# An attention and MLP kernel on one core: its work items broken into single instructions, with a newly written order

## The chip, the cores and the metric

The kernel runs on one core of one Trainium2 chip. The metric is the device time of one execution in microseconds (us), as the median of several runs. The core has five engines that run side by side, each through its own queue in the order written: PE (TensorE: matmul and transpose), DVE (VectorE), ACT (ScalarE), POOL (GpSimd) and SP (SyncE, which here issues all DMAs). An engine whose next instruction waits for another engine does nothing else meanwhile.

## The reference

Inputs are q, k, v of shape (4, 8, 576, 64), a tiny network that makes a position bias, and the weights of an MLP with 512 inputs and 2048 hidden units. All is float32.

```python
scores = scale * np.matmul(q, k.transpose(0, 1, 3, 2))
x = (psi_rel / psi_i)[..., None]          # log1p|i-j| / log1p(max(i,1))
h = np.maximum(x @ w1 + b1, 0.0)          # 32 hidden units
bias = h @ w2                             # one value per (i, j, head)
scores = scores + bias.transpose(2, 0, 1)[None, :, :, :]
attn = exp(scores - max); attn = attn / (sum + 1e-09)
attn_out = np.matmul(attn, v)             # then (B*S, H*D) = (2304, 512)
h = np.maximum(x @ w_in, 0.0)
out = h * h @ w_out
```

## The kernel before

Every float32 operand of a large matmul is split into a float16 high part and a float16 rest, and three float16 matmuls take the place of one float32 matmul. The work is cut into items, and `PROGRAM` is a list of words, each naming one item (kind and numbers). The kinds:

- Bias: `hg:g.j` (min or max of a table row, on DVE and ACT, L444 and L440) makes the hidden layer for group g of 16 rows, `bm:g.c` multiplies it by w2 on PE (L501), `bo` writes it out of PSUM (ACT L520, DVE L525) and by DMA to `biasd` in DRAM, and `bl:n` loads the slice of step n. There are 36 groups.
- Weights: `wd:i` loads a piece of 128 x 512 double-precision words, `ws:i` makes float16 halves of it: three steps on DVE (L348, L349, L351), a cast on ACT (L260), a scale and a subtraction on POOL. There are 32 pieces; MLP unit u of every block needs pieces 4u to 4u+3.
- Attention: 80 steps n, one head of two batches and up to 128 rows each. `qk:n` makes scores in the one PSUM buffer `sc` (PE L561, L566, L571), `sa:n` adds the bias and takes the maximum on DVE (L588, which frees `sc` for the next step) and the exponential on ACT (L597), then the weights are transposed: in steps 0 to 15 by PE (`tu:n.b`, L610 and L615, copied out of PSUM by ACT, L611 and L616), later by DMA after a split on ACT and POOL (`sb:n`). `pv:n` multiplies by V on PE (L660; float32 in steps 0 to 15, where each such matmul leaves two records in the trace). `po:k` divides four heads' results by the sums (DVE L674, L676).
- MLP: ten blocks of eight steps each. `no:k` scales a block (DVE L691 and others), `tx:k.b` splits it on DVE (L704, L705) and transposes it by DMA, `g1:n` is the first matmul of unit n (24 records, L719), `sq:n` squares with relu (ACT L732, DVE L733, DVE L264, POOL L736), `g2:n` the second matmul (12 matmuls, 6 in the half blocks, L750), `ou` stores.

Two PSUM buffers `h` serve `bm`, `tu` and `g1` in turn: the third of them can begin only when the first has been copied out. Buffers are handed out in the order of the words.

After all instructions are recorded, a table `STREAMS` holds a permutation of each engine's instructions (PE 5712, ACT 693, DVE 692, POOL 385, SP 376), and a chain of order-only dependences fixes that order. So engine order is already free of the words' order; the buffers are not. The core of it:

```python
for word in PROGRAM.split():
    kind, _, arg = word.partition(":")
    work[kind](*[int(x) for x in arg.split(".") if x])
...
        for prev, i in zip(seq, seq[1:]):
            tc.add_manual_dep(i, prev.name, mybir.DependencyInfo(
                mybir.DependencyClass.NoSync, mybir.DependencyReason.DATA), reason="order")
```

Of the kernel before, what the change touches and what calls it, by code (L numbers as in the profile page):

```python
# [44 lines left out]
NF = 2  # L45
PROGRAM = (
    "st tb:0 qd:0 tb:1 wd:0 wd:1 sc hc kd:0.0 hg:0.0 wd:2 hg:0.1 kd:0.1 hg:1.0 vd:0.0 vd:0.1 hg:2.0 hg:1.1 vd:0.2 "
    "bm:0.1 vd:0.3 hg:2.1 vd:0.4 bm:1.1 vd:0.5 qs:0 vd:0.6 bo:0.1.0 hg:3.0 hg:3.1 rs bm:0.0 bo:0.0.0 bm:1.0 ks:0.0 "
    "bm:2.0 vd:0.7 bm:2.1 bo:1.0.0 bo:1.1.0 bm:3.1 bo:2.0.0 bm:3.0 ks:0.1 bo:2.1.0 kz:0.0 qk:0 kd:0.2 bo:3.0.0 "
    "bo:3.1.0 qd:1 ws:0 hg:4.0 hg:4.1 bm:4.0 kz:0.1 kd:0.3 ws:1 wd:3 hg:5.0 hg:5.1 bm:5.0 bo:4.0.0 bo:4.0.1 wd:4 "  # L50
    "bo:5.0.0 bo:5.0.1 ws:2 hg:6.0 hg:6.1 bm:6.0 ks:0.2 bl:0 bl:1 wd:5 kz:0.2 bo:6.0.0 bl:2 qs:1 bo:6.0.1 hg:7.0 "
    "kd:0.4 ks:0.3 ws:3 qd:2 hg:7.1 bm:7.0 kz:0.3 kd:0.5 wd:6 sa:0 bo:7.0.0 bo:7.0.1 ws:4 qk:1 bl:3 hg:8.0 hg:8.1 "
    "sa:1 tu:0.0 wd:7 bl:4 ws:5 tu:0.1 tu:1.0 ks:0.4 wd:8 tu:1.1 qk:2 kz:0.4 kd:0.6 bm:8.0 ks:0.5 sa:2 pv:0 "
    "bo:8.0.0 pv:1 bo:8.0.1 ws:6 bl:5 hg:9.0 qk:3 hg:9.1 wd:9 tu:2.0 qs:2 kd:0.7 kz:0.5 sa:3 tu:2.1 bm:9.0 bl:6 "
    "qk:4 bo:9.0.0 bo:9.0.1 ws:7 pv:2 ks:0.6 hg:10.0 qd:3 hg:10.1 bm:10.0 wd:10 kz:0.6 sa:4 tu:3.0 bo:10.0.0 bl:7 "
    "bo:10.0.1 ws:8 tu:3.1 hg:11.0 hg:11.1 qk:5 pv:3 po:0 wd:11 ws:9 bm:11.0 sa:5 ks:0.7 qk:6 bo:11.0.0 tu:4.0 "
    "bo:11.0.1 wd:12 ws:10 tu:4.1 sa:6 pv:4 hg:12.0 qk:7 hg:12.1 wd:13 bm:12.0 qs:3 kz:0.7 bl:8 tu:5.0 bl:9 "
    "bo:12.0.0 qd:4 tu:5.1 bo:12.0.1 ws:11 tu:6.0 sa:7 wd:14 ws:12 qk:8 hg:13.0 hg:13.1 bl:10 tu:6.1 pv:5 bm:13.0 "
    "pv:6 sa:8 wd:15 bo:13.0.0 tu:7.0 bo:13.0.1 ws:13 hg:14.0 tu:7.1 qk:9 bl:11 hg:14.1 pv:7 wd:16 bm:14.0 sa:9 "
    "tu:8.0 bo:14.0.0 tu:8.2 bo:14.0.1 ws:14 qk:10 bl:12 hg:15.0 hg:15.1 wd:17 tu:8.1 bm:15.0 sa:10 po:1 bo:15.0.0 "  # L60
    "ws:15 bo:15.0.1 wd:18 ws:16 qk:11 hg:16.0 bl:13 hg:16.1 bm:16.0 qs:4 wd:19 tu:9.0 qd:5 bo:16.0.0 bo:16.0.1 "
    "ws:17 tu:9.2 no:0 hg:17.0 tu:9.1 hg:17.1 wd:20 ws:18 tu:10.0 tu:10.2 pv:8 vs:0.0 sa:11 wd:21 ws:19 tx:0.0 "
    "tu:10.1 pv:9 ws:20 wd:22 bl:14 bm:17.0 tu:11.0 bo:17.0.0 wd:23 vs:0.1 tu:11.2 bo:17.0.1 ws:21 qk:12 hg:18.0 "
    "hg:18.1 tu:11.1 wd:24 g1:0 sa:12 bm:18.0 sq:0 ws:22 pv:10 bo:18.0.0 bl:15 bo:18.0.1 ws:23 wd:25 hg:19.0 "
    "hg:19.1 tu:12.0 g1:1 wd:26 vs:0.2 tu:12.1 sq:1 ws:24 qk:13 wd:27 tu:12.2 sa:13 bm:19.0 g2:0 bo:19.0.0 "
    "bo:19.0.1 ws:25 hg:20.0 g1:2 wd:28 hg:20.1 qk:14 bl:16 sq:2 ws:26 g1:3 g2:1 sq:3 sa:14 wd:29 tu:13.0 ws:27 "
    "pv:11 po:2 vs:0.3 bl:17 wd:30 ws:28 tu:13.1 qk:15 tu:13.2 wd:31 bm:20.0 sa:15 g2:2 bo:20.0.0 qs:5 bo:20.0.1 "
    "ws:29 hg:21.0 tu:14.0 bl:18 hg:21.1 tu:14.1 pv:12 vs:0.4 kd:1.0 ws:30 qd:6 qk:16 g2:3 ws:31 kd:1.1 tu:14.2 "
# [795 lines left out]
```

## Time and profile before

| what | value |
|---|---|
| median of 3 runs | 653.91 us (653.08 to 658.23) |
| the profiled execution's own time | 654.47 us |
| its span in the trace | 652.5 us |
| mean granted PE clock | 0.963 |
| busy PE / DVE / ACT / POOL | 616.6 / 417.1 / 380.0 / 379.5 us |

The span is what the trace covers; 2.0 us of the execution's own time lie around it. A busy time is the union of an engine's instructions. [...]

### The profile page before, as it was taken

What the parts mean: (1) busy time and instruction counts of PE and PEld (TensorE: products, weight loads), DVE (VectorE), ACT (ScalarE), POOL (GpSimd) and SP (SyncE); (2) the same over time, 40 slices, a digit from 0 to 9 for tenths busy, and PEclk for the clock granted to TensorE, in tenths of its full rate; (3) what the DMA queues carried; (4) which work ended last, traced back from release to release, by engine and by line L of the source; (5) the groups of instructions that cost most, each with busy time, mean ns of one, the idle gap of its engine ahead of it and who ended that gap; (6) DMA issues with size and microseconds to landing.
All of it is one profiled execution on the core that took longest, in us unless ns stands there. A gap on an engine that the chain in (4) does not pass through costs nothing.

```text
span 652.5 us, 15566 instructions
## 1 busy us (share of the span) xinstructions
PE 616.6 (94%) x6056; PEld 398.4 (61%) x6056; DVE 417.1 (64%) x836; ACT 380.0 (58%) x838; POOL 379.5 (58%) x389
## 2 busy tenths in 40 slices
PE   5686889989999999999999999999999999999997
PEld 2143366756666647666666666766766666767664
DVE  8878987967977895596784456437445642632321
ACT  7689977975854457657654655655565563342111
POOL 5777467998465447678884545647455655342221
PEclk9779968978999999999999999999999999999999
DMA  8999886746996799999977867777787677624000
GB/s 316 305 309 287 288 259 188 245 127 129 187 209 163 149 194 206 162 190 226 255 164 145 188 120 168 156 162 147 149 167 145 147 143 147 131 58 79 17 34 16
DMA packets 206568, 112.16 MB, mean 172 GB/s; under 512 B 167072, under 2 KB 183456, under 8 KB 206496
## 3 DMA queue, kind: packets, MB, share of 16 engines
q1 hardware_dynamic: 206496, 111.19, 72.7%
q8 instruction: 47, 0.77, 0.5%
q14 instruction: 25, 0.20, 0.1%
HBM read 55.44 MB, written 15.61 MB: 109 GB/s over the span
## 4 chain that ended last, share of the span: by engine, by line
PE 63%; DVE 13%; DMA 8%; ACT 8%; issue 4%; POOL 3%; SPq 0%; DVEq 0%; POOLq 0%; ACTq 0%
PE hp L719 23%; PE o L750 22%; PE pv L660 9%; PE sc L571 5%; DMA at<-a 3%; PE bp L501 2%; DVE s L588 2%; DVE hg L444 2%; ACT s L597 2%; POOL a L629 2%; DMA biasd<-be 2%; ACT be L520 1%; ACT hg L440 1%; PE sc L566 1%; DMA stg<-w_in 1%
## 5 line engine op out<-in xcount | busy, mean ns | idle before, releaser
L719 PE MATMUL hp<-xt,winH 128*128 128x256 f16 (+1 forms) x1280 | 195.8, 263 | 0.1
L750 PE MATMUL o<-woutH,g 128*128 128x512 f16 x576 | 185.7, 379 | 0.4 <-POOL g L736 0.4
L736 POOL TENSOR_TENSOR g<-r,g 128x512 f16<-128x512 f32 (+1 forms) x80 | 90.9, 1136 | 139.2 <-DVE g L264 110.0
L719 PE MATMUL hp<-xt,winL 128*128 128x256 f16 (+1 forms) x640 | 162.9, 263 | 0.0
L588 DVE CUSTOM_DVE_ANT_0 s<-sc,bt 128x576 f32<-128x576 f32 x144 | 104.5, 750 | 58.3 <-PE sc L571 25.2
L750 PEld LDWEIGHTS <-g 128*128 128x128 f16 x864 | 82.2, 98 | 92.9 <-issue 8.3
L719 PEld LDWEIGHTS <-winH 128*128 128x128 f16 x1280 | 117.3, 98 | 31.4 <-issue 13.0
L629 POOL TENSOR_TENSOR a<-s,a 128x1024 f16<-128x1024 f32 (+1 forms) x64 | 131.1, 2049 | 0.0
L733 DVE TENSOR_TENSOR r<-hp,r 128x512 f32<-128x512 f32 (+1 forms) x80 | 50.8, 636 | 117.1 <-ACT r L732 116.9
L597 ACT ACTIVATE s<-s,nm 128x576 f32<-128x576 f32 x144 | 111.5, 775 | 6.7
L750 PE MATMUL o<-woutL,g 128*128 128x512 f16 x288 | 109.2, 379 | 0.0
L596 ACT ACTIVATE nm<-mx,esc 128x1 f32<-128x1 f32 x144 | 40.8, 288 | 114.3 <-DVE mx L588 113.8
L660 PE MATMUL pv<-v,at 128*128 128x64 f16 (+5 forms) x2112 | 97.1, 208 | 3.8 <-ACT at L611 3.0
L732 ACT ACTIVATE r<-hp 128x512 f32<-128x512 f32 (+1 forms) x80 | 43.6, 544 | 72.9 <-PE hp L719 72.8
L260 ACT ACTIVATE a<-s 128x1152 f16<-128x1152 f32 (+1 forms) x64 | 70.3, 1098 | 21.0 <-DMA at<-a 20.3
L660 PEld LDWEIGHTS <-at 128*128 128x128 f16 (+1 forms) x1792 | 56.7, 100 | 19.0 <-issue 6.3
L719 PEld LDWEIGHTS <-winL 128*128 128x128 f16 x640 | 63.1, 99 | 5.8
L628 POOL TENSOR_TENSOR a<-s,a 128x128 f16<-128x128 f32 (+1 forms) x64 | 28.5, 445 | 49.0 <-ACT a L260 47.2
L444 DVE TENSOR_SCALAR hg<-tab_t 128x464 f32<-128x464 f32 (+17 forms) x84 | 54.9, 684 | 2.5 <-PE bp L501 2.4
L571 PE MATMUL sc<-k,q 64*128 64x512 f16 x384 | 53.7, 386 | 0.0
L501 PE MATMUL bp<-hg,w2s 128*32 128x288 f32 (+16 forms) x156 | 35.8, 546 | 9.7 <-ACT hg L440 6.5
L660 PEld LDWEIGHTS pv<-v,at 128*64 128x64 f32 (+3 forms) x320 | 33.1, 197 | 11.4 <-ACT at L611 4.1
(88 smaller groups left out, 701.8 us busy)
## 6 DMA issues: line engine op xcount, KB each, us to landing
bt<-biasd SPq DMA_DIRECT2D x64, 288.0 KB, 3.3
stg<-w_in SPq DMA_DIRECT2D x16, 512.0 KB, 5.2
stg<-w_out SPq DMA_DIRECT2D x16, 512.0 KB, 4.8
bt<-biasd SPq DMA_DIRECT2D x32, 144.0 KB, 4.4
qst<-qd SPq DMA_DIRECT2D x32, 128.0 KB, 3.4
out<-o SPq DMA_DIRECT2D x16, 256.0 KB, 2.3
v<-vd SPq DMA_DIRECT2D x8, 320.0 KB, 6.4
stg<-vd SPq DMA_DIRECT2D x8, 320.0 KB, 4.1
```

Of the source, the lines that this page charges most:

```text
L260: nc.scalar.activation(out=out, in_=in_, func=AF.Copy, scale=scale)
L444: nc.vector.tensor_scalar(ht, src, scl[:, n:n + 1], None, op0=ALU.min)
L501: nc.tensor.matmul(out=bp[32 * t:32 * t + 32, 0:n], lhsT=w2s if gi < 4 or t < z else w2n, rhs=hg[gi, t][:, a0:a1, :] if gi in ONEP else hg ...
L571: nc.tensor.matmul(out=sc[:, 1024 * b:1024 * b + 512], lhsT=qt[r, qz, qs], rhs=kt[r, z, 64 * b:64 * b + 512], start=(m == 0), stop=(m == 2 ...
L588: nc.vector.tensor_tensor_reduce(s[:, 576 * b:576 * b + 576], sc[:, 960 * sb:960 * sb + 576], bt, inv, -3.0e38, ALU.add, ALU.max, mx[:, b: ...
L597: nc.scalar.activation(out=sl, in_=sl, func=AF.Exp, bias=nm[:, b:b + 1], accum_out=su[:, h, b:b + 1])
L629: eng.tensor_tensor(av[:, :, 640:1152], ev[:, :, 0:512], av[:, :, 0:512], op=ALU.subtract)
L660: nc.tensor.matmul(out=dst, lhsT=lhsT, rhs=vt[r, 5 * b + blk, :] if f32 else vt[:, vz, 5 * b + blk, :], start=(m == 0), stop=(m == nt - 1) ...
L719: nc.tensor.matmul(out=hp[:, f * T:f * T + T].rearrange("p (b t) -> p b t", b=nb), lhsT=wt[:, k, c0:c0 + 128], rhs=xt[:, 0:nb, z * 4 + k, ...
L733: nc.vector.tensor_tensor(rr, hp[:, 0:2 * T], rr, op=ALU.mult)
L736: eng.tensor_tensor(g[:, 1, 0:2 * T], rr, g[:, 0, 0:2 * T], op=ALU.subtract)
L750: nc.tensor.matmul(out=blk["o"][b], lhsT=g[:, z, c0:c0 + 128], rhs=wt[:, 2 * u + f, :], start=(u == 0 and f == 0 and z == 0 and wt is wout ...
```

## The change

Each item function becomes a generator that stops (`yield`) after an instruction. A word of `PROGRAM` now runs one such unit: the first time it stands there it starts the item, each later time it runs the item's next unit. Most units are one instruction; a run of matmuls (`qk`, `pv`, `g1`, half a `g2`) is still one unit. `PROGRAM` is therefore much longer, `STREAMS` is gone, and each engine runs its instructions in the order in which the words bring them. Buffers are now taken when the unit that first writes them stands in the list. Which engine does what is as before, and so are the pools.

The list `f32c` of the two blocks that use float32 in `pv` becomes a count of steps, `NF = 16`: the same steps. Their `po` now carries V's power of two through the sums (one more tiny constant, `eps[:, 1:2]`, and a scale in an ACT instruction that was there before).

```diff
-NF = 2
+NF = 16
 PROGRAM = (
...
+    "st tb:0 qd:0 st st tb:1 st st st st st st st wd:0 qd:0 qd:0 qd:0 sc hc hc kd:0.0 hc hc hc hc hc kd:0.1 sc rs "
...
-STREAMS = {
-    "PE": (
...
     def softmax_a(n):
...
             nc.vector.tensor_tensor_reduce(
                 s[:, 576 * b:576 * b + 576],
                 sc[:, 960 * sb:960 * sb + 576], bt, inv, -3.0e38, ALU.add, ALU.max, mx[:, b:b + 1])
+            yield
...
     def pv(n):
...
-        f32 = (p, c) in f32c
+        f32 = n < NF
...
     def pv_out(k):
...
+        f32 = 4 * k < NF
+        nc.scalar.activation(out=rd[:, :, 0:nb], in_=su[:, h0:h0 + 4, 0:nb], func=AF.Identity,
+                             scale=float(2.0 ** -VS) if f32 else 1.0, bias=eps[:, 1:2] if f32 else eps[:, 0:1])
+        yield
...
     def square(n):
...
-        g = g_p.tile([128, 2, 512], F16, tag="g", name="g")
         rr = r[:, 0:2 * T]
         nc.scalar.activation(out=rr, in_=hp[:, 0:2 * T], func=AF.Relu, scale=float(2.0 ** (-2 * RS)))
+        yield
         nc.vector.tensor_tensor(rr, hp[:, 0:2 * T], rr, op=ALU.mult)
+        yield
+        g = blk["g"][u] = g_p.tile([128, 2, 512], F16, tag="g", name="g")
...
+    live = {}
     for word in PROGRAM.split():
-        kind, _, arg = word.partition(":")
-        work[kind](*[int(x) for x in arg.split(".") if x])
...
+        if word not in live:
+            kind, _, arg = word.partition(":")
+            live[word] = iter(work[kind](*[int(x) for x in arg.split(".") if x]) or ())
+        next(live[word], None)
```

What the new list does to the order shows at two places. The first is PE's queue at the first steps of the second block. Before, behind `qk:11`: bias group 16 (L501), `tu:9` (L610, L615), the first transposes of `tu:10`, `pv:8` (L660), a last `tu:10`, `pv:9`.

```order
L501 MATMUL bp_1143<-hg_1135,w2s_130 32x384 x2
L501 MATMUL bp_1143<-hg_1140,w2n_132 32x384 x2
L610 MATMUL tp_1154<-ident_140,s_1025 128x128 x4
L615 MATMUL tp_1177<-ident_140,s_1025 64x128 x2
L610 MATMUL tp_1192<-ident_140,s_1025 128x128 x4
L610 MATMUL tp_1212<-ident_140,s_1089 128x128 x4
L615 MATMUL tp_1218<-ident_140,s_1089 64x128 x2
L660 MATMUL pv_1222<-v_193,at_1034 128x64 x10
L610 MATMUL tp_1261<-ident_140,s_1089 128x128 x4
L660 MATMUL pv_1222<-v_195,at_1153 128x64 x10
```

After, the same engine from `tu:8.1` on (L667 and L674 are the transposes, L723 is `pv`, L547 the bias, L615 and L620 `qk`). Up to the first weight load of `qk:11`:

```order
L667 MATMUL tp_1087<-ident_140,s_970 128x128 x4
L723 MATMUL pv_1105<-v_184,at_1066 128x64 x10
L547 MATMUL bp_1128<-hg_1094,w2s_130 32x384 x2
L547 MATMUL bp_1128<-hg_1097,w2n_132 32x384 x2
L667 MATMUL tp_1137<-ident_140,s_1043 128x128 x4
L674 MATMUL tp_1148<-ident_140,s_1043 64x128 x2
L615 LDWEIGHTS q_624
```

and from the end of `qk:11` on, with `tu:9.1`, `pv:9`, bias group 17, `tu:10` and `pv:10`:

```order
L620 MATMUL sc_141<-k_411,q_624 128x512
L667 MATMUL tp_1173<-ident_140,s_1043 128x128 x4
L723 MATMUL pv_1105<-v_192,at_1153 128x64 x10
L547 MATMUL bp_1212<-hg_1185,w2s_130 32x368 x2
L547 MATMUL bp_1212<-hg_1201,w2n_132 32x368 x2
L667 MATMUL tp_1227<-ident_140,s_1123 128x128 x4
L674 MATMUL tp_1235<-ident_140,s_1123 64x128 x2
L667 MATMUL tp_1247<-ident_140,s_1123 128x128 x4
L723 MATMUL pv_1105<-v_202,at_1240 128x64 x10
```

`pv:8` now stands ahead of bias group 16 and directly behind its own transposes, `qk:11` (nine matmuls) stands between the two halves of `tu:9`, and `tu:10` comes after `pv:9`.

The second place is DVE's queue where the softmax of steps 16 to 18 meets the first unit of the second MLP block. Before: the last step of `ws:31` (L351), the two halves of step 16 (L588 on `s_1841`, with three bias rows L444 between them), both halves of step 17 (`s_1924`), then the product of `sq:4` (L733).

```order
L351 SCALAR_TENSOR_TENSOR cv_1822<-stg_1718,ci_1823 128x512
L588 ISA s_1841,mx_1842<-sc_142,bt_1587 128x576
L588 ISA mx_1842 128x1
L444 TENSOR_SCALAR hg_1869<-tab_t_129 128x432
L444 TENSOR_SCALAR hg_1872<-tab_t_129 128x432 x2
L588 ISA s_1841,mx_1842<-sc_142,bt_1587 128x576
L588 ISA mx_1842 128x1
L588 ISA s_1924,mx_1925<-sc_142,bt_1687 128x576
L588 ISA mx_1925 128x1
L588 ISA s_1924,mx_1925<-sc_142,bt_1687 128x576
L588 ISA mx_1925 128x1
L733 TENSOR_TENSOR r_1976<-hp_1940,r_1976 128x256
```

After: `sq:4` (L808) stands ahead, then the last weight steps, bias group 23, the product of `sq:5`, and only then the first half of step 17 (L637 on `s_2022`).

```order
L808 TENSOR_TENSOR r_1923<-hp_1879,r_1923 128x256
L380 SCALAR_TENSOR_TENSOR cv_1940<-stg_1775,ci_1911 128x512
L373 TENSOR_SCALAR ci_1945<-stg_1850 128x512
L375 SCALAR_TENSOR_TENSOR ci_1945<-stg_1850,ci_1945 128x512
L482 TENSOR_SCALAR hg_1955<-tab_t_129 128x448
L380 SCALAR_TENSOR_TENSOR cv_1987<-stg_1850,ci_1945 128x512
L482 TENSOR_SCALAR hg_2002<-tab_t_129 128x448 x2
L743 TENSOR_TENSOR x_1463<-pv_1585,rd_1828 128x256
L808 TENSOR_TENSOR r_2008<-hp_1958,r_2008 128x256
L743 TENSOR_TENSOR x_1463<-pv_1585,rd_1828 128x256
L637 ISA s_2022,mx_2023<-sc_141,bt_1694 128x576
L637 ISA mx_2023 128x1
```

On PE the same place reads, in words, `tu:15.0 tu:15.1 qk:17 tu:15.2 pv:14 g1:4 bm:22 qk:18 g1:5 bm:23 pv:15` before, and `pv:14 qk:16 g2:3 tu:15.1 tu:15.0 tu:15.2 g1:4 bm:22 pv:15 g1:5 qk:17 bm:23` after. From step 40 on the two orders on PE agree but for a few units that change places with near ones.

## Rows read from the trace of the kernel before

**Rows 1.** Busy time of each engine by stage, to 640 us; PEclk is the granted clock.

```profile
core 0: us, PE busy (x) PEld busy (x) DVE busy (x) ACT busy (x) POOL busy (x), PEclk, DMA share, GB/s
0.00:20.00 20.00, 11.56 (x102) 5.31 (x102) 17.29 (x42) 13.43 (x27) 10.09 (x21) 1.00 0.92 328
20.00:40.00 20.00, 13.96 (x48) 4.53 (x46) 14.62 (x25) 13.80 (x33) 14.69 (x16) 0.60 1.00 290
40.00:80.00 40.00, 31.27 (x326) 16.37 (x322) 36.87 (x75) 37.29 (x92) 24.48 (x27) 0.95 0.95 301
80.00:103.00 23.00, 19.30 (x93) 14.39 (x91) 17.54 (x36) 16.13 (x39) 13.89 (x17) 0.63 0.72 214
103.00:136.00 33.00, 32.95 (x303) 23.27 (x302) 31.28 (x59) 26.66 (x64) 31.02 (x41) 1.00 0.74 219
136.00:158.00 22.00, 19.51 (x133) 13.48 (x133) 12.95 (x24) 14.77 (x32) 19.84 (x23) 0.77 0.43 106
158.00:330.00 172.00, 170.10 (x1805) 107.67 (x1805) 134.47 (x258) 105.79 (x233) 111.60 (x105) 1.00 0.92 195
330.00:640.00 310.00, 310.00 (x3195) 208.58 (x3192) 150.61 (x318) 150.67 (x320) 151.84 (x139) 1.00 0.62 127
```

**Rows 2.** Timeline of PE, 81 to 104 us: start, duration, instruction, idle time before it.

```profile
85.17 1.93 PE L610 MATMUL tp<-ident,s 128*128 128x128 f32 x8 [2.32 <-ACT be L520]
...
88.40 4.94 PE L660 MATMUL pv<-v,at 128*128 128x64 f32 x20
93.27 1.11 PE L610 MATMUL tp<-ident,s 128*128 128x128 f32 x4
```

**Rows 3.** Timeline of PE, 104 to 124 us: the same kinds of instruction later.

```profile
105.88 2.86 PE L660 MATMUL pv<-v,at 128*128 128x64 f32 x20
108.67 0.66 PE L610 MATMUL tp<-ident,s 128*128 128x128 f32 x4
```

**Rows 4.** Timeline of ACT, 82 to 85 us.

```profile
82.74 0.79 ACT L597 ACTIVATE s<-s,nm 128x576 f32<-128x576 f32 x1
...
83.50 0.65 ACT L260 ACTIVATE winH<-cv 128x512 f16<-128x512 f32 x1
84.02 1.10 ACT L520 ACTIVATE be<-bp,hcst,rows_s 128x207 f32<-128x207 f32 x2
```

**Rows 5.** The chain of waits, 136 to 160 us: start, duration, what.

```profile
142.49 4.73 PE pv L660 x20
147.22 2.68 PE hp L719 x24
149.90 0.98 PE bp L501 x8
150.88 0.27 PE sc L566 x3
151.15 0.75 PE sc L571 x6
151.90 1.45 PE hp L719 x24
153.35 2.23 PE bp L501 x8
155.58 2.79 PE pv L660 x20
```

**Rows 6.** Who waited for whom, 136 to 158 us: total, times, longest.

```profile
DVE r L733 <- ACT r L732: 6.4, 1, 6.4
...
PE sc L566 <- DVE mx L588: 1.6, 1, 1.6
```

**Rows 7.** What DVE waited for, 20 to 44 us: total, times, longest.

```profile
DVE ci L348 <- DMA stg<-w_out: 3.6, 1, 3.6
DVE q L395 <- POOL q L262: 2.6, 1, 2.6
```

**Rows 8.** Groups of instructions by line and shape: busy time, mean ns of one.

```profile
L351 DVE SCALAR_TENSOR_TENSOR cv<-stg,ci 128x512 uint32<-128x512 uint32 x32 | 21.7, 678 | 0.8 <-DMA biasd<-be 0.5
```

More of the change, by code (lines that the diff above doesn't have):

```diff
@@ L44 @@
 NKZ = 8
-NF = 2
+NF = 16
 PROGRAM = (
[67 rows of a table removed]
-)
-NAMES = {"PE": "PE", "Activation": "ACT", "DVE": "DVE", "Pool": "POOL", "SP": "SP"}
-STREAMS = {
-    "PE": (
-        "0-3 12-19 4-11 20-980 987-1014 981-986 1015-1065 1072-1095 1066-1071 1096-1360 1367-1375 1361-1366 1376-1526 "
-        "1533-1536 1527-1532 1537-2083 2090-2113 2084-2089 2114-2667 2674-2697 2668-2673 2698-3251 3258-3281 3252-3257 "
-        "3282-3835 3842-3865 3836-3841 3866-4419 4426-4449 4420-4425 4450-5711 "
-    ),
-    "ACT": (
[15 rows of a table removed]
-    ),
-    "DVE": (
[16 rows of a table removed]
-    ),
-    "POOL": (
[8 rows of a table removed]
-    ),
[11 rows of a table removed]
-    ),
-}
[153 rows of a table added]
+)
 @with_exitstack
@@ L273, in tile_attention_moe @@
         groups += list(range(32, 36)) if c == 0 else list(range(8 * c - 8, 8 * c))
-    f32c = order[:NF]
     k_t, v_t, q_t, kst, vst, wst, q_st = {}, {}, {}, {}, {}, {}, {}
@@ L577, in softmax_a @@
         bt = b_t.pop(n)
[L578 removed]
+        s = s_t[n] = s_p.tile([128, 1152], F32, tag="w", name="s")
         mx = sml.tile([128, 2], F32, tag="mx", name="mx")
         nm = sml.tile([128, 2], F32, tag="nm", name="nm")
[L581 removed]
+        if (p, c) not in sums:
             sums[p, c] = sml.tile([128, H, 2], F32, tag="sum", name="sum")
@@ L603, in turn, with at_of @@
         e = s_t[n]
-        if b == 0:
-            at_t[n] = as_f32(at_p.tile([128, 20, 128], F16, tag="at", name="at")).rearrange("p (k i) -> p k i", i=128)
-        at = at_t[n]
+        def at_of():
+            if n not in at_t:
+                t = as_f32(at_p.tile([128, 20, 128], F16, tag="at", name="at"))
+                at_t[n] = t.rearrange("p (k i) -> p k i", i=128)
+            return at_t[n]
         if b < nb:
@@ L666, in pv_out @@
         h0 = k % 2 * 4
-        po = pv_t.pop(k)
-        if h0 == 0:
+        su = sums[p, c]
+        rd = sm2.tile([128, 4, 2], F32, tag="rd", name="rd")
+        f32 = 4 * k < NF
+        nc.scalar.activation(out=rd[:, :, 0:nb], in_=su[:, h0:h0 + 4, 0:nb], func=AF.Identity,
+                             scale=float(2.0 ** -VS) if f32 else 1.0, bias=eps[:, 1:2] if f32 else eps[:, 0:1])
+        yield
+        nc.vector.reciprocal(out=rd[:, :, 0:nb], in_=rd[:, :, 0:nb])
+        yield
+        po = pv_t[k]
+        if (p, c) not in x_t:
             x_t[p, c] = x_p.tile([128, 2, DM], F32, tag="x", name="x")
         x = x_t[p, c]
-        su = sums[p, c]
-        rd = sm2.tile([128, 4, 2], F32, tag="rd", name="rd")
-        nc.scalar.activation(out=rd[:, :, 0:nb], in_=su[:, h0:h0 + 4, 0:nb], func=AF.Identity, bias=eps)
-        nc.vector.reciprocal(out=rd[:, :, 0:nb], in_=rd[:, :, 0:nb])
         for b in range(nb):
@@ L743, in g2 @@
         g = blk["g"].pop(u)
-        if u == 0:
-            blk["o"] = [ps_o.tile([128, 512], F32, tag=f"o{b}", name=f"o{b}") for b in range(nb)]
         for b in range(nb):
+            if u == 0:
+                blk["o", b] = ps_o.tile([128, 512], F32, tag=f"o{b}", name=f"o{b}")
             for f in range(2):
@@ L749, in g2 @@
                     c0 = f * T + b * 128
-                    nc.tensor.matmul(out=blk["o"][b], lhsT=g[:, z, c0:c0 + 128], rhs=wt[:, 2 * u + f, :],
+                    nc.tensor.matmul(out=blk["o", b], lhsT=g[:, z, c0:c0 + 128], rhs=wt[:, 2 * u + f, :],
                                      start=(u == 0 and f == 0 and z == 0 and wt is woutH),
                                      stop=(u == 7 and f == 1 and z == 1))
+            if b < nb - 1:
+                yield
     def store(k, b):
@@ L758, in store @@
         if zn("oe", 2 * k + b) == "A":
-            nc.scalar.activation(out=o, in_=blk["o"][b], func=AF.Copy, scale=blk["os"][:, b:b + 1])
+            nc.scalar.activation(out=o, in_=blk["o", b], func=AF.Copy, scale=blk["os"][:, b:b + 1])
         else:
-            nc.vector.tensor_scalar(o, blk["o"][b], blk["os"][:, b:b + 1], None, op0=ALU.mult)
+            nc.vector.tensor_scalar(o, blk["o", b], blk["os"][:, b:b + 1], None, op0=ALU.mult)
+        yield
         if c:
@@ L779, in start @@
                                 compare_op=ALU.is_equal, fill=0.0)
+        yield
         if "T" in ENG["wl"]:
             nc.gpsimd.tensor_scalar(negw, ident, -float(2.0 ** -WIS), 1.0, op0=ALU.mult, op1=ALU.mult)
-        nc.vector.memset(eps, 1.0e-9 * 2.0 ** ESC)
+            yield
+        nc.vector.memset(eps[:, 0:1], 1.0e-9 * 2.0 ** ESC)
+        yield
+        nc.vector.memset(eps[:, 1:2], 1.0e-9 * 2.0 ** (ESC - VS))
+        yield
         nc.vector.memset(esc, ESC * LN2)
+        yield
         nc.scalar.activation(out=nb1, in_=hcst[:, 0:1], func=AF.Exp)
@@ L802, in tile_attention_moe @@
             "ou": store}
+    live = {}
     for word in PROGRAM.split():
-        kind, _, arg = word.partition(":")
-        work[kind](*[int(x) for x in arg.split(".") if x])
-    own = {e: [] for e in STREAMS}
-    for i in nc.cur_bb.bb.instructions:
-        e = NAMES.get(str(i.engine).split(".")[-1])
-        if e and type(i).__name__.startswith("Inst"):
-            own[e].append(i)
-    for e, text in STREAMS.items():
-        seq = []
-        for w in text.split():
-            a, _, b = w.partition("-")
-            seq += own[e][int(a):int(b or a) + 1]
-        assert len(seq) == len(own[e])
-        for prev, i in zip(seq, seq[1:]):
-            tc.add_manual_dep(i, prev.name, mybir.DependencyInfo(
-                mybir.DependencyClass.NoSync, mybir.DependencyReason.DATA), reason="order")
+        if word not in live:
+            kind, _, arg = word.partition(":")
+            live[word] = iter(work[kind](*[int(x) for x in arg.split(".") if x]) or ())
+        next(live[word], None)
+    tail = {}
+    for i in nc.cur_bb.bb.instructions:
+        if type(i).__name__.startswith("Inst"):
+            e = str(i.engine)
+            if e in tail:
+                tc.add_manual_dep(i, tail[e].name, mybir.DependencyInfo(
+                    mybir.DependencyClass.NoSync, mybir.DependencyReason.DATA), reason="order")
+            tail[e] = i
 def kernel(q, k, v, w1, b1, w2, moe_w_in, moe_w_out):
```

95 lines of the change are left out of this document (75 added, 20 removed), and 269 rows, old and new, of tables (PROGRAM, STREAMS).

## The prediction

> **What bounds the kernel now.** I read the busy times by stage first [rows 1]. From 330 to 640 us PE is busy in every microsecond at a granted clock of 1.00, and from 158 to 330 us it lacks 1.9 us in 172. The work of PE does not change, so nothing is to be had in these 482 us but those 1.9; whatever the new order does there, PE has to run through the same matmuls, and DVE, ACT and POOL each have half their time left (150 to 152 us of 310). All that an order can win lies ahead of 158 us. [...]
>
> What PE waits for there is not one engine. From 40 to 80 us DVE (36.9 of 40) and ACT (37.3 of 40) are both nearly full, and the DMA share is 0.95; from 20 to 40 it is 1.00, and DVE waits 3.6 us for a weight load and 2.6 us for a cast on POOL [rows 1, 7]. These stretches are full of work, and I expect little there. The stretches 80 to 103 and 136 to 158 are different: no engine is full (DVE 17.5 of 23 and 13.0 of 22, ACT 16.1 and 14.8), and PE is slow. In the first, PE pauses 2.32 us for ACT's copying out of bias group 16, which frees the PSUM buffer for the next transposes; then eight transposes take 1.93 us, `pv:8` 4.94 us, and another four transposes 1.11 us [rows 2]. The same `pv` takes 2.86 us and the same four transposes 0.66 us at 105 to 109 us [rows 3]. In the second, the chain runs over PE alone: `pv:14` 4.73 us against 2.79 for `pv:15`, `g1:4` 2.68 against 1.45 for `g1:5`, bias group 23 2.23 against 0.98 for group 22 [rows 5]. Meanwhile DVE sits 6.4 us behind the product of `sq:4`, whose matmul stands behind the slow `pv:14`, and `qk:17` had waited 1.6 us for DVE [rows 6]. So here idle time makes a slow clock, and the slow PE makes the others idle.
>
> **The change part by part.** The time of the profiled execution is 654.47 us; its span is 652.5, so 1.97 us lie around it, and the median of the runs, 653.91, is 0.56 below it. A new span counts as itself plus 1.4.
>
> *V's power of two* costs nothing: the same 16 steps use float32 as before, the scale sits in an ACT instruction that was there, and one memset of a single column is added on DVE in the first 3 us, where DVE waits for loads anyway (it is busy 17.3 of 20 [rows 1]). With that cover gone it is one tiny instruction.
>
> *Units in place of items, and buffers taken later* add no instruction to any engine. They matter only through the order, so I price the order at the two places where PE is slow.
>
> *80 to 103 us.* The pause of 2.32 us ended when ACT had copied out bias group 16 at 84.02 us. Ahead of that on ACT stood an exponential of step 10 (from 82.74 to 83.50, 0.76 us) and a weight cast (to 84.02, 0.52 us) [rows 4]. In the new order these two come behind; another cast of the same size (0.52) and a transpose copy of about as much take 1.0 us of their 1.28, so the copying out comes 0.3 us sooner. And PE now has `qk:11` to do between the two halves of `tu:9`: three and six matmuls, 0.27 + 0.75 = 1.02 us [rows 5]. The pause falls to about 2.32 - 1.02 - 0.3 = 1.0 us; regained 1.3. The slow clock behind the pause cost 2.08 us in each of two `pv` (4.94 - 2.86; the second, `pv:9`, has the same 4.94), 0.45 in each of two groups of four transposes (1.11 - 0.66), and 0.6 in the eight (1.93 - 2 x 0.66): 5.7 us [rows 2, 3]. I take it that with `pv:8` ahead of bias group 16 and the pause at 1.0 us the clock holds: 7.0 us for this place. If it falls all the same, 1.3; if the new pauses are no shorter, 0.
>
> [...]
>
> *136 to 158 us.* Before, `qk:17` stood directly behind `tu:15.1` and waited 1.6 us for DVE's second half of step 16 [rows 6]. In the new order PE has `pv:14`, `g1:4`, bias group 22, `pv:15` and `g1:5` ahead of it: 2 x 2.79 + 2 x 1.45 + 0.98 = 9.5 us more work at the full clock [rows 5]. On DVE six steps of the last two weight pieces now come behind step 16, 6 x 0.68 = 4.1 us less ahead of it [rows 8]. So the wait goes, and so does DVE's wait of 6.4 us, since `g1:4` is no longer behind step 17. The slow clock there cost 1.94 + 1.23 + 1.25 = 4.4 us in the three groups above. Other pauses can make the clock fall here, since PE only just became dense, so I take half, 2.2, with the 1.6: 3.8 us. The ends are 0 and 6.0.
>
> What is late next: in the new order `sa:0` and `sa:1` stand seven DVE instructions further back, behind bias groups 8 and 9, and the last weight steps come the 4.1 us later that were counted above. Unit 7 of the first MLP block needs them, and `tu:15`, `g1:4` to `g1:6` and two `pv` still stand ahead of it on PE, so there is room. POOL, which halves the weights and V behind DVE, is nearly full from 103 to 158 us (31.0 of 33, 19.8 of 22 [rows 1]), and nobody in these rows waits long for it. New pauses of PE somewhere I price between 0 (as from 103 to 136, where PE misses 0.05 us in 33) and 5 us; from 40 to 80 us it misses 8.7 in 40, but that stretch exists already. PE's work there grows denser, at the former rate; I take 1.5.
>
> Sum: 652.5 - 7.0 - 3.8 + 1.5 = 643.2 us of span, **644.6 us**.
>
> **The rivals.** *All pauses but the forced ones go.* DVE is idle 158 - (17.3 + 14.6 + 36.9 + 17.5 + 31.3 + 13.0) = 27.4 us ahead of 158 [rows 1]. Forced are 2.7 at the start, the 6.2 for the loads and the cast [rows 7], and 3.1 from 40 to 80 us. If DVE, the engine with the most work there, paces the new order without other gaps, 15.4 us go: a span of 637.1, 638.5 us. For it: PE's work ahead of DVE's at the second place shrinks as shown. Against it: ACT is as full as DVE from 40 to 80.
>
> *The waits only move.* The old order was already set for each instruction of each engine, so the units give no freedom but that of the buffers. The clock falls at other places for as long; only the second place is better: 3.8 us gained and up to 5 lost, a span of 648.7 to 653.7, 650 to 655 us. For it speaks that the stretches to 80 us are full, and that PE's share of busy time ahead of 103 us is low in any order.
>
> *Slower: one more fall of the clock.* PE ran 103 to 136 us at 1.00 with hardly a pause [rows 1]. The new order moves `tu:10`, `tu:12` and `pv:11` to `pv:13` against `g1` and `g2` in just this stretch. If a pause like the 2.32 us arises there, a third slow stretch costs what the first did, 5.7 + 2.3 = 8.0 us, and if the first one stays and the second gains nothing, the span is 660.5, 661.9 us. It decides from a pause of some 2 us that is followed by a `pv` of more than 4 us. Against it: ACT (26.7 of 33) has room there.
>
> **How the numbers follow.** The forecast has a chance of 0.50, all pauses gone 0.15, waits that only move 0.22, one more fall of the clock 0.13. The forecast's own range is 639 to 650 (the 7.0 down to 1.3, the 3.8 up to 6.0, new pauses 0 to 5, not all at once). The range over all reaches from 634, a little under the first rival since part of the load waits could go too, to 656, which takes in the moved waits and leaves out the third rival. A measurement of this kernel can tell about 1% from no change, 6.5 us. Faster by more than that (under 647.4): nine tenths of the forecast and the first rival, 0.60. Within 1%: 0.27. Slower by over 1%: 0.13.
>
> **What would show it.** Right if the clock of the stretch around `pv:8` and `pv:9` is near 1.00 and both take about 2.8 us; if `qk:17` waits for nothing and DVE has no wait of 6 us at `sq:4`; if the 310 us of full PE stand unchanged, only earlier; and if the stretch to 80 us is as before within 2 us. Wrong if a `pv` of float32 steps still takes 4.9 us, if PE pauses for ACT's copying out at other steps, or if DVE waits longer for weight loads ahead of 80 us.

## The result and the profile after

The changed kernel takes 647.28 us (median of 4, 646.23 to 648.05) against 654.25 for the kernel before on the same chip: a ratio of 0.9882 (of the means of the runs), 95% interval 0.9838 to 0.9926. On another chip it was 647.25 against 655.88, 0.9875 (0.9840 to 0.9911). The forecast was 644.6 in a range of 634 to 656. The profiled execution has a span of 645.6 us, 6.9 less than before.

The busy times by stage, which answer to [rows 1] (columns: stretch, its length, busy time and instructions of PE, PEld, DVE, ACT and POOL, granted clock (1.00 is the full clock), DMA share, GB/s):

```profile
0.00:20.00 20.00, 10.69 (x94) 5.07 (x94) 16.44 (x41) 13.10 (x27) 8.87 (x21) 1.00 0.92 321
20.00:40.00 20.00, 12.03 (x38) 2.65 (x38) 16.75 (x27) 12.13 (x27) 14.96 (x17) 0.61 1.00 305
...
80.00:103.00 23.00, 20.67 (x191) 15.68 (x190) 21.82 (x45) 21.58 (x54) 21.52 (x25) 1.00 0.83 239
103.00:136.00 33.00, 31.57 (x276) 21.73 (x275) 29.64 (x57) 26.73 (x63) 31.18 (x41) 1.00 0.71 213
136.00:158.00 22.00, 18.88 (x178) 9.81 (x178) 21.09 (x36) 15.27 (x33) 19.38 (x24) 1.00 0.65 159
158.00:180.00 22.00, 19.14 (x214) 11.80 (x211) 15.77 (x33) 17.90 (x39) 12.42 (x12) 1.00 0.99 204
```

The two slow stretches are gone: the clock from 80 to 103 us is 1.00 (0.63 before), from 136 to 158 us 1.00 (0.77). The slow one from 20 to 40 us stays, at 0.61. The other engines do more in the same time: DVE is busy 21.8 of 23 us in the first (17.5 before) and 21.1 of 22 in the second (13.0). From 330 to 640 us PE is full as before.

The timeline of PE around `pv:8` and `pv:9`, which answers to [rows 2, 3] (the kernel before had 4.94 us for each):

```profile
78.83 1.36 PE L723 MATMUL pv<-v,at 128*128 128x64 f32 x10
80.40 1.47 PE L723 MATMUL pv<-v,at 128*128 128x64 f32 x10 [0.21 <-ACT at L670]
82.58 0.66 PE L667 MATMUL tp<-ident,s 128*128 128x128 f32 x4
...
84.80 1.36 PE L723 MATMUL pv<-v,at 128*128 128x64 f32 x10
86.48 1.47 PE L723 MATMUL pv<-v,at 128*128 128x64 f32 x10 [0.31 <-ACT at L670]
```

Each `pv` is 2.83 us of work (1.36 + 1.47), with a pause of 0.2 or 0.3 us in it, and four transposes take 0.66 us. What PE waited for from 136 to 180 us (total, times, longest), to be read beside [rows 6]:

```profile
PE pv L723 <- DMA at<-a: 2.9, 2, 1.9
PE o L827 <- POOL g L814: 1.8, 2, 1.0
PE o L827 <- POOL g L281: 1.0, 1, 1.0
PE bp L547 <- DVE hg L482: 0.3, 1, 0.3
```

The wait of `qk:17` for DVE is gone, and so is DVE's wait of 6.4 us. In their place PE waits for POOL's halves of the squares and for the transposes by DMA of steps 17 and 19. At the head, the first softmax half of step 0 on DVE (L588 in the kernel before, L637 in the changed one, 0.75 us in both) begins at 31.52 us before and at 37.23 us now.

It comes 5.7 us later. To see what that is worth, and where the 6.9 us came from, I use PE's lag: the time less the work that PE has done by then, where each group of matmuls counts at what it takes undisturbed (of its kind and per matmul, the duration that a quarter of the groups in the traces of before and after stay under). Idle time and a slow clock both add to the lag; work moved about does not, and idle transposes count as no work. In us, with some of the experiments below:

| at | before | changed | e1 old order | e2 first place undone | e3 second undone | e4 old head | e5 old order, pauses filled | e8 first place alone |
|---|---|---|---|---|---|---|---|---|
| 40 | 18.9 | 20.7 | 19.8 | 20.7 | 20.2 | 19.9 | 19.9 | 20.3 |
| 80 | 30.8 | 30.6 | 31.8 | 31.8 | 30.4 | 30.9 | 32.5 | 29.7 |
| 103 | 42.3 | 33.2 | 43.6 | 43.7 | 33.0 | 37.8 | 40.4 | 32.9 |
| 136 | 42.3 | 34.7 | 44.9 | 46.2 | 41.7 | 38.7 | 41.7 | 41.7 |
| 158 | 49.8 | 39.1 | 51.2 | 48.8 | 48.2 | 43.8 | 45.1 | 48.7 |
| 180 | 50.2 | 43.2 | 52.1 | 55.9 | 52.4 | 46.4 | 47.8 | 49.8 |
| 640 | 54.6 | 47.7 | 56.2 | 61.7 | 57.0 | 52.5 | 51.6 | 53.8 |

Against the kernel before, the changed one is level at 80 us (0.2 ahead), gains 8.9 from 80 to 103, loses 1.5 to 136, gains 3.1 to 158 and loses 3.7 to 180; 6.9 remain at the end, the difference of the two spans.

Each column is one execution. In the trace of e9, which is the changed kernel again in an execution of 650.50 us, PE is busy 32.68 us from 40 to 80 us against 35.82 here, so the lag at 80 us can differ by some 3 us between executions of one kernel; from 80 to 103 and from 136 to 158 us the clock is 1.00 there too. The columns e4 and e8 are of executions of 652.15 and 653.86 us, above their medians.

### The profile page after: what moved, and what is told of

Read it like the earlier page. It is cut to its first block, busy times and chain, and to the rows that moved or that the text cites. A ratio compares the mean times of both kernels' runs of the same rounds, so it can differ in the third digit from the quotient of the medians.

```text
span 645.6 us, 15577 instructions
## 1 busy us (share of the span) xinstructions
PE 608.3 (94%) x6056; PEld 388.9 (60%) x6056; DVE 421.3 (65%) x837; ACT 380.9 (59%) x838; POOL 378.3 (59%) x389
## 4 chain that ended last, share of the span: by engine, by line
PE 71%; DMA 9%; ACT 9%; POOL 4%; issue 3%; DVE 3%; SPq 0%; DVEq 0%; POOLq 0%; ACTq 0%
PE o L827 26%; PE hp L794 24%; PE pv L723 8%; PE sc L620 5%; DMA at<-a 4%; PE bp L547 3%; ACT s L649 2%; DMA xt<-xh 2%; ACT be L566 2%; PE sc L610 1%; ACT hg L478 1%; DMA qst<-qd 1%; PE sc L615 1%; DMA stg<-w_out 1%; ACT at L670 1%
## 5 line engine op out<-in xcount | busy, mean ns | idle before, releaser
L814 POOL TENSOR_TENSOR g<-r,g 128x512 f16<-128x512 f32 (+1 forms) x80 | 87.0, 1088 | 116.4 <-DVE g L283 88.3
L637 DVE CUSTOM_DVE_ANT_0 s<-sc,bt 128x576 f32<-128x576 f32 x144 | 104.7, 749 | 46.3 <-PE sc L620 28.8
L808 DVE TENSOR_TENSOR r<-hp,r 128x512 f32<-128x512 f32 (+1 forms) x80 | 50.8, 635 | 120.0 <-ACT r L806 119.9
L723 PE MATMUL pv<-v,at 128*128 128x64 f16 (+5 forms) x2112 | 90.4, 204 | 3.4 <-DMA at<-a 2.9
L723 PEld LDWEIGHTS <-at 128*128 128x128 f16 (+1 forms) x1792 | 56.2, 100 | 20.6 <-issue 7.6
L620 PE MATMUL sc<-k,q 64*128 64x512 f16 x384 | 52.6, 379 | 0.0
L547 PE MATMUL bp<-hg,w2s 128*32 128x288 f32 (+16 forms) x156 | 39.0, 547 | 12.4 <-ACT hg L478 9.0
L283 DVE TENSOR_SCALAR g<-r 128x512 f16<-128x512 f32 (+1 forms) x64 | 38.5, 601 | 2.5 <-DVE r L808 0.5
```

The costliest lines, as they stand in the source:

```text
L547: nc.tensor.matmul(out=bp[32 * t:32 * t + 32, 0:n], lhsT=w2s if gi < 4 or t < z else w2n, rhs=hg[gi, t][:, a0:a1, :] if gi in ONEP else hg ...
L620: nc.tensor.matmul(out=sc[:, 1024 * b:1024 * b + 512], lhsT=qt[r, qz, qs], rhs=kt[r, z, 64 * b:64 * b + 512], start=(m == 0), stop=(m == 2 ...
L637: nc.vector.tensor_tensor_reduce(s[:, 576 * b:576 * b + 576], sc[:, 960 * sb:960 * sb + 576], bt, inv, -3.0e38, ALU.add, ALU.max, mx[:, b: ...
L723: nc.tensor.matmul(out=dst, lhsT=lhsT, rhs=vt[r, 5 * b + blk, :] if f32 else vt[:, vz, 5 * b + blk, :], start=(m == 0), stop=(m == nt - 1) ...
L808: nc.vector.tensor_tensor(rr, hp[:, 0:2 * T], rr, op=ALU.mult)
L814: eng.tensor_tensor(g[:, 1, 0:2 * T], rr, g[:, 0, 0:2 * T], op=ALU.subtract)
```

## The experiments

Theory A: the time is in the order of the engines; at two places it removes the pauses of PE behind which the clock fell. Rival B: taking the buffers later is what gains. Rival C: the later start of step 0 is carried to the end, so that the gain could have been larger. The first four ran on one chip, the next four on another, the last four on a third, each set beside the kernel before. Every run that changes the order moves units of all engines together; none changes PE's order alone.

**e1, the old order in the new units.** The list is sorted so that each engine runs as before (up to a few tiny instructions); units, later buffers and V's power of two stay. On PE, at the first place (- the changed list, + this one, the words of PE alone):

```diff
-tu:8.1 pv:8 bm:16.0 tu:9.0 tu:9.2 qk:11 tu:9.1 pv:9 bm:17.0 tu:10.0
+tu:8.1 bm:15.0 qk:11 bm:16.0 tu:9.0 tu:9.2 tu:9.1 tu:10.0 tu:10.2 pv:8
```

> The changed program (single units, buffers taken at the unit, V's power of two), but its list is sorted so that every engine runs its instructions in the order of the kernel before. Theory A (the time is all in the order of the engines): 652 to 656 us, as before, with the slow pv of 4.9 us at 88 us. Rival B (taking the buffers later is what gains): 647 to 650 us, with shorter pauses in the old order.

Measured: 656.19 us, 1.0028 of before (1.0004 to 1.0053), at the upper end of what theory A gave. B fell: the units and the buffers gain nothing by themselves. The timeline of PE has the old pause and the old slow `pv:8`:

```profile
78.82 0.53 PE L546 MATMUL bp<-hg,w2s 128*32 128x400 f32 x2 [1.21 <-ACT at L669]
...
80.37 0.33 PE L614 MATMUL sc<-kz,q 128*128 128x128 f16 x3 [0.68 <-DVE mx L636]
...
82.84 1.02 PE L546 MATMUL bp<-hg,w2s 128*32 128x384 f32 x3 [1.38 <-ACT hg L477]
...
84.12 0.66 PE L666 MATMUL tp<-ident,s 128*128 128x128 f32 x4
...
87.19 1.14 PE L666 MATMUL tp<-ident,s 128*128 128x128 f32 x8 [2.20 <-ACT be L565]
...
90.44 4.94 PE L722 MATMUL pv<-v,at 128*128 128x64 f32 x20
```

**e2, the first place undone; e3, the second undone.** In the changed list the units between `pv:7` and `pv:11` (e2), or between `pv:13` and the first half of `g2:5` (e3), go back into their old relative order. e2 has on PE what the diff of e1 shows; e3:

```diff
-pv:14 qk:16 g2:3 tu:15.1 tu:15.0 tu:15.2 g1:4 bm:22.0 pv:15 g1:5 qk:17
+qk:16 g2:3 tu:14.2 bm:21.0 tu:15.0 tu:15.1 qk:17 tu:15.2 pv:14 g1:4
```

> The changed kernel with the units between pv:7 and pv:11 put back into the relative order of before (PE: qk:11, bm:16, tu:9, tu:10, then pv:8); the rest of the list as changed. Theory A (the clock falls behind the pause for bias group 16): pv:8 and pv:9 take 4.9 us again and the time is 5 to 9 us above the changed kernel, 652 to 656 us. Rival (the pause was made further ahead, by the order up to pv:7): pv:8 stays at 2.9 us and the time within 2 us of the changed kernel, 645 to 649 us.

> The changed kernel with the units between pv:13 and the first half of g2:5 put back into the relative order of before (qk:17 directly behind tu:15.1). Theory A: qk:17 waits for DVE again, and the time is 2 to 4 us above the changed kernel, 649 to 651 us. Rival (POOL, busy without a gap from 124 to 150 us in the changed kernel, sets when the second block's units come, whatever PE's order): within 1 us of the changed kernel, 646 to 648 us.

Measured: e2 660.60 us, 1.0091 of before (1.0059 to 1.0123); e3 656.71 us, 1.0040 (1.0011 to 1.0068). Both lose more than the whole gain, and both lie above the range that either theory gave. In e2, PE's waits from 80 to 103 us and its `pv`:

```profile
PE tp L666 <- ACT be L565: 2.2, 1, 2.2
PE sc L614 <- DVE mx L636: 1.6, 1, 1.6
PE tp L673 <- ACT s L648: 1.5, 1, 1.5
```

```profile
90.55 4.94 PE L722 MATMUL pv<-v,at 128*128 128x64 f32 x20
96.33 4.93 PE L722 MATMUL pv<-v,at 128*128 128x64 f32 x20
108.83 2.86 PE L722 MATMUL pv<-v,at 128*128 128x64 f32 x20
```

The slow `pv:8` and the lag at 103 us, 43.7 against 33.2, are as theory A has them, and the rival of e2 fell. But behind 158 us the lag grows by another 12.9 us to the end, against 8.6 in the changed kernel and 4.8 in the kernel before; from 158 to 180 us PE waits 3.1 us for POOL and 2.0 for a transpose by DMA. That the rest of the list was planned for engines that are further on may be why; no run shows it. e3, PE's timeline:

```profile
128.15 0.48 PE L614 MATMUL sc<-kz,q 128*128 128x128 f16 x3 [2.97 <-DVE mx L636]
...
137.09 1.12 PE L666 MATMUL tp<-ident,s 128*128 128x128 f32 x4 [2.23 <-ACT be L565]
...
140.90 4.94 PE L722 MATMUL pv<-v,at 128*128 128x64 f32 x20
```

Here the units of the old order come as a block behind a new prefix, so that the pauses of 2.97 and 2.23 us are larger than what stood there before; the slow `pv:14` behind them is the old one. The rival of e3 (POOL sets the pace there whatever PE does) fell, since the order does count. How much of the 9.5 us is the second place and how much the new seam was not separated.

**e4, the old head.** All units that ran before 80 us go into the old order, the rest as changed.

> The order of before for all units that ran there before 80 us, then the changed order for the rest. In the changed kernel the second softmax half of step 0 comes 5.7 us later than before. Theory A (the full stretch from 40 to 80 us takes that up; PE had done the same work by 80 us in both): 646 to 649 us. Rival C (the late start is carried to the end): 641 to 643 us.

Measured: 650.86 us, 0.9952 (0.9920 to 0.9984), slower than the changed kernel. Step 0 starts early again (its first softmax half is what moved by 5.7 us, where the expectation says the second), yet at 80 us the lag is 30.9, as in both kernels, so C fell: the stretch from 40 to 80 us takes the late start up. But the time is not that of the changed kernel: in the new surroundings PE pauses 1.19, 0.69 and 0.48 us, and `pv:8` is slow:

```profile
77.52 0.53 PE L546 MATMUL bp<-hg,w2s 128*32 128x400 f32 x2 [1.19 <-ACT at L669]
...
79.09 0.33 PE L614 MATMUL sc<-kz,q 128*128 128x128 f16 x3 [0.69 <-DVE mx L636]
...
81.16 5.10 PE L722 MATMUL pv<-v,at 128*128 128x64 f32 x20 [0.48 <-DVE x L742]
```

This is the profiled execution. The ten executions of e4 run from 648.31 us, at a mean clock of 0.989, to 657.99 us, at 0.965, and the time follows the clock: how long the clock is low differs between executions of one order.

**e5, the pauses of the old order filled.** e1 with idle transposes of the identity into a part of the scores' PSUM tile that nobody reads:

```diff
+    def filler(i, m):
+        for _ in range(m):
+            nc.tensor.transpose(sc[:, 576:704], ident, ident)
```

> The old order in single units, as in the first experiment, with 26 idle transposes of the identity added on PE in three pauses: 7 ahead of bias group 16, 12 ahead of tu:9.1, 7 ahead of the last transposes of tu:10 (some 4.3 us of work in 4.95 us of pauses; their output is read by nobody). Theory A (PE's idling there is what lowers the clock): pv:8 and pv:9 take 2.8 to 3.0 us in place of 4.87, and the time falls by 3 to 7 us against the old order in units, to 649 to 653 us. Rival (the clock falls for another reason, or the slow pv are hidden by another engine): pv:8 at 4.9 us, or the time within 1.5 us of 656.

Measured: 651.96 us, 0.9959 (0.9937 to 0.9980); 0.7% or 4.2 us under e1, by adding work. PE's timeline:

```profile
82.38 0.98 PE L895 MATMUL sc<-ident 128*128 128x128 f32 x7
...
85.83 1.47 PE L895 MATMUL sc<-ident 128*128 128x128 f32 x12
...
89.16 0.93 PE L895 MATMUL sc<-ident 128*128 128x128 f32 x7
...
91.35 2.76 PE L722 MATMUL pv<-v,at 128*128 128x64 f32 x20
...
94.54 2.76 PE L722 MATMUL pv<-v,at 128*128 128x64 f32 x20
```

Order, buffers and data are those of e1; PE has work in three pauses, its idle time from 80 to 103 us falls from 5.42 to 4.20 us (0.89 of the pause of 2.20 us are left), the clock there rises from 0.68 to 1.00, and `pv:8` takes 2.76 in place of 4.94 us. That the idling at this place lowers the clock, and that the low clock costs time at the end, is shown by this run. Not all of the 4.2 us is won there: the lag grows by 7.9 us from 80 to 103 us where e1 has 11.8, and from 136 to 158 us, where nothing was filled, by 3.4 where e1 has 6.3. The wait of `qk:17` for DVE is 1.62 us there (1.63 in e1), but the clock of that stretch is 0.92 against 0.77, and `pv:14` is slow for a part only:

```profile
139.08 0.48 PE L614 MATMUL sc<-kz,q 128*128 128x128 f16 x3 [1.62 <-DVE mx L636]
...
141.31 3.32 PE L722 MATMUL pv<-v,at 128*128 128x64 f32 x20
```

By the lag the low clock cost 7.5 and 3.7 us in the two stretches that are no longer slow in the changed kernel (worked out in the next section), 1.7% of the span.

**e6, the head of the changed kernel filled** in the same way, in six pauses from 18 to 64 us.

> The changed kernel with 44 idle transposes of the identity in PE's pauses between 18 and 64 us (7, 14, 8 and 8 ahead of bias groups 5 to 8, 2 ahead of tu:2.0, 5 ahead of tu:6.0; nobody reads their output). Theory A (up to 80 us DVE, ACT and the DMAs set the time, so a faster clock of PE buys nothing): granted clock from 20 to 40 us up from 0.61 to 0.8 or more, time within 1.5 us of the changed kernel, 646 to 649 us. Rival (the slow clock lengthens the chain over PE there): 642 to 645 us.

Measured: 646.19 us, 0.9872 (0.9850 to 0.9893), the same as the changed kernel. The clock rose from 0.61 to 0.92 in the stretch from 20 to 40 us:

```profile
20.00:40.00 20.00, 12.53 (x67) 5.22 (x64) 16.74 (x27) 11.58 (x25) 14.88 (x18) 0.92 1.05 302
```

So in this kernel the slow clock ahead of 40 us costs nothing that can be measured. From 18 to 45 us of the changed kernel PE waits 7.5 us for ACT's hidden rows and ACT 2.6 us for PE's bias matmuls; why the faster clock buys nothing there was not separated.

**e7, V's first cast from POOL to ACT; e10, hidden rows from DVE to ACT.** Both take work from an engine that is nearly full from 136 to 158 us:

```diff
-"vh": "PPPPPPPAPPPPPPPP"
+"vh": "PAAAAAAAPPPPPPPP"
-HID = "112222222222222222222211111111000000"
+HID = "112222222222222222222212222211000000"
```

(The first pair is e7, the second e10.)

> The changed kernel with the first cast of V for heads 1 to 6 (0.75 us each) given from POOL to ACT; POOL has 4.5 us less to do between 90 and 150 us. Theory A (POOL, on the chain of waits nearly without a gap from 124 to 150 us, sets when the squares of the first MLP block are ready, and PE's 2.8 us of waits for them are part of the loss): 643 to 646 us. Rival (ACT, with the copying out of the transposes behind these casts, takes POOL's place): 647 to 650 us.

> The changed kernel with one hidden row of each of bias groups 23 to 27 moved from DVE to ACT (five rows; DVE's rows of this kind take 0.5 to 2.2 us between 138 and 165 us, where a POOL subtraction runs beside them). Theory D (DVE, busy 21.1 of 22 us from 136 to 158 us and stretched by POOL, is what the second place waits for): 643 to 646 us. Rival (the loss from 136 to 180 us is set by the transposes by DMA, issued by SP one after another): within 1 us of the changed kernel.

Measured: e7 646.49 us, 0.9884 (0.9854 to 0.9913); e10 646.63 us, 0.9867 (0.9834 to 0.9900). Neither can be told from the changed kernel; e7 lies between the two ranges given, e10 in that of its rival. In e7 PE's waits for POOL stand at the very same 2.8 us:

```profile
PE pv L722 <- DMA at<-a: 2.8, 2, 2.0
PE o L826 <- POOL g L813: 1.8, 2, 1.0
PE o L826 <- POOL g L280: 1.0, 1, 1.0
```

But POOL was not simply relieved: from 80 to 160 us it now waits 3.1 us for ACT's casts of V, for which it did not wait in the changed kernel. So e7 does not settle whether POOL's amount of work sets those waits; it shows that this way of taking work off POOL doesn't pay. In e10 DVE is busy 18.45 us from 136 to 158 us in place of 21.09, PE 18.35 instead of 18.88, and PE's waits for POOL are 3.7 us: less work on DVE does not end them.

**e8, the first place alone.** The changed order up to `pv:11`, the order of before for the rest.

> The changed order for all units up to pv:11 (106 us), the order of before for the rest: the first place alone. Theory A (the first place gives 9 us by itself): 645 to 649 us, with qk:17 waiting for DVE and a slow pv:14 as before. Rival (what is gained by 106 us is given back in the old rest, whose engines are not there sooner): 650 to 655 us.

Measured: 651.33 us, 0.9960 (0.9935 to 0.9985). The rival held: 3.2 us of gain are left in the medians. In the profiled execution, a long one of 653.86 us, the 9.4 us of lag that are won at 103 us shrink to 0.6 at 136 us. PE's timeline:

```profile
106.03 1.09 PE L666 MATMUL tp<-ident,s 128*128 128x128 f32 x4 [3.51 <-DVE r L807]
...
138.91 0.33 PE L614 MATMUL sc<-kz,q 128*128 128x128 f16 x3 [1.85 <-DVE mx L636]
...
140.92 4.94 PE L722 MATMUL pv<-v,at 128*128 128x64 f32 x20
```

From 103 to 136 us PE waits 4.9 us for DVE; `pv:14` is slow as before. The pause of 3.51 us lies at the seam of the two orders, so a part of this loss belongs to the seam.

**e9, the changed kernel again, e11 and e12, the additions together.** e11 has e6 and e7, e12 the rows of e10 as well.

> The changed kernel unaltered, timed on the same chip as the next three. All theories: 646 to 649 us, 0.988 of the kernel before.

> The changed kernel with both the 44 idle transposes up to 64 us and V's first cast on ACT. If their small gains are real and add (1 us each): 644.5 to 646 us. If they are noise: within 1 us of the changed kernel on the same chip.

> The kernel of the run before this one with the five hidden rows on ACT as well. Theory D: 641 to 644 us. Rival: as the run before this one, or 1 to 2 us slower since ACT now has both the casts and the rows.

Measured: 647.25, 648.10 and 649.32 us; 0.9875 (0.9840 to 0.9911), 0.9892 (0.9860 to 0.9924) and 0.9905 (0.9871 to 0.9939). The small gains do not add; none of these versions beats the changed kernel. In the traces of e11 and e12 the clock from 80 to 103 us is 0.85, where e6, e7 and the changed kernel have 1.00, though in e11 PE is idle for less of that stretch (1.39 us against 2.33) and no wait there is over 0.6 us. Why it fell there is open.

## Why the prediction was right, and where its sizes were off

- *The units, the buffers and V's power of two cost nothing.* e1 bears it out nearly: in the old order they give 1.0028 of before, between 0.3 and 3.5 us slower by the interval.
- *The first place, 7.0 us.* The mechanism was right, shown from both sides by e2 (`pv:8` of 4.94 us behind the pause) and e5 (2.76 us with the pauses filled). It measured 8.9 us in the lag. One reading was off without touching the sum: ACT began to copy out bias group 16 at 84.02 us and took 1.10 us [rows 4]; it had not ended then. PE's idle time from 80 to 103 us fell from 3.70 us (23 less 19.30 [rows 1]) to 2.33, 1.4 against the 1.3 of the forecast. The slow clock gave back the other 7.5, where I had summed 5.7: I had counted the `pv` and the transposes, and not bias group 17 and the other matmuls up to 102 us.
- *The second place, 3.8 us.* 3.1 measured, and that these are near is luck, since both parts were off. The waits named did go, and the clock there is 1.00, but 3.1 us of idle time took the place of 2.5: I had 1.6 us won there, and 0.6 were lost, to POOL. The other 3.7 us came from the clock, where I had taken 2.2, half of 4.4. The 4.4 holds a misreading: bias group 23 [rows 5] ran at the full clock. Its 2.23 us were two waits of PE for DVE's hidden rows, the last of which came at 154.60 us. The kernel before, busy times and clock as above, behind the slow part:

```profile
150.10:158.00 7.90, 7.90 (x68) 4.43 (x60) 7.50 (x12) 4.63 (x11) 6.36 (x8) 1.00 0.61 126
```

  That the pauses lower the clock was tested by filling them at the first place alone; at the second it is argued from e3.
- *New pauses, 1.5 us.* This is the term that was mis-sized: 1.5 us from 103 to 136 and 3.7 from 158 to 180 us, 5.2 together, just beyond the range that I gave (0 to 5). From 103 to 136 us PE waits 1.4 us for ACT's copying out of transposes, which I had named as a sign of being wrong. POOL was on my list of what is late next, but I wrote that nobody waits long for it; the 2.8 us of waits for its halves of the squares are what spoils the second place. From 158 to 180 us PE waits 2.9 us for two transposes by DMA, which were not on the list, in a stretch where the DMA share is 0.99 and where PE had not missed anything before. PE, SP's issue of step 17's transpose, and the chain of waits:

```profile
160.15 0.99 PE L723 MATMUL pv<-v,at 128*128 128x64 f16 x28 [0.93 <-DMA at<-a]
...
177.72 0.99 PE L723 MATMUL pv<-v,at 128*128 128x64 f16 x28 [1.93 <-DMA at<-a]
```

```profile
155.39 3.16 SPq L695 DMA_TRANSPOSE at<-a  x1
```

```profile
170.00 7.67 DMA at<-a
```

  Step 17's transpose is issued 0.03 us after POOL's subtraction ends (153.24 + 2.12 = 155.36, shown in the last section), and lands 4.72 us later. Step 19's is issued 3.0 us after its subtraction, when SP has issued four other transfers, and takes 7.67 us. They land at 160.10 and 177.67 us, where the kernel before has 163.38 and 181.52: they do come sooner, by 3.3 and 3.9 us, but PE is 10.7 us further on at 158 us. Why the second takes 7.67 us was not settled, and no run moves these transposes.
- *The stretch to 80 us as before within 2 us* held at its end in the profiled execution (0.2 us of lag; some 3 more in e9's), though step 0 starts 5.7 us later; e4 shows that this start is taken up by 80 us, and e6 that the clock from 20 to 40 us does not count.
- *"The waits only move"* was wrong for the list as a whole, but e8 and e3 show what was right in it: half of the new order does not keep its half of the gain. I had added up the two places as if each stood alone. Undone one by one they cost 13.4 (e2) and 9.5 us (e3) against 647.25 (timed on another chip; by the ratios 14 and 10), the seams included; the first alone gives 3.2. The sum of the prediction came within 2.4 us of the gain because 1.9 us more at the first place stood against 0.7 less at the second and 3.7 more of new pauses; that much is luck.

## What to carry to other kernels

Where PE runs at a low clock in a stretch, it paid here to look for the pauses ahead of it (from 80 to 103 us the clock was 0.68 in e1, and 1.00 in e5 with three pauses filled) and to price them with what follows at the low clock, not by themselves; a few idle matmuls in those pauses tested the cause and were worth 4.2 us, though in the head of the changed kernel (e6) they gained nothing that can be measured. An order planned as a whole need not be a sum of local changes: undone in parts, this one lost more than the parts had given. What is regained runs into the next limit, here POOL's queue and the transposes by DMA (2.8 and 2.9 us of PE's waits), so the price of what is late next belongs to the transfers as much as to the engines.

## What the runs showed of the hardware that I had not expected

A row of DVE's hidden layer, one SBUF input of 128 x 480 float32, takes 0.42 us alone (0.84 for two) and 2.23 us when a subtraction of POOL runs beside it; it ends 0.27 us behind that subtraction. DVE and POOL in the changed kernel:

```profile
153.40 2.23 DVE L482 TENSOR_SCALAR hg<-tab_t 128x480 f32<-128x480 f32 x1
...
156.23 0.84 DVE L482 TENSOR_SCALAR hg<-tab_t 128x480 f32<-128x480 f32 x2
```

```profile
153.24 2.12 POOL L692 TENSOR_TENSOR a<-s,a 128x1024 f16<-128x1024 f32 x1
```

The subtraction ends at 153.24 + 2.12 = 155.36, and the row at 155.63. Three more rows of the same trace, of 2.32, 1.20 and 2.26 us, end 0.26 to 0.28 us behind such a subtraction. What holds the rows back, the trace doesn't show. Against the 0.42 us of a row alone, some 1.8 us of this one came on top, an estimate from the two times; so DVE's busy time of 21.1 us there overstates its work.

The other surprise is that the length of a pause does not tell by itself whether the clock falls. In e4 pauses of 1.19, 0.69 and 0.48 us were followed by a `pv` of 5.10 us. In e1 there are pauses of 1.21, 0.68 and 1.38 us at the same place, and the four transposes behind them still took 0.66 us, as at a clock of 1.00; behind the 2.20 us that came next and one more pause of 1.37, `pv:8` took 4.94. In e5 a wait of 1.62 us was followed by a `pv` of 3.32 us, in e1 at the same place one of 1.63 by 4.94. What decides was not found, and the prediction's "pause of some 2 us" is no bound.
